# Output tiles turned by VectorE in blocks of 32 and stored in runs of 64 channels, in place of TensorE transposes and ScalarE copies

## The chip, the cores and the metric

The kernel runs on one core of a Trainium2 chip. The metric is the device time of one execution in microseconds; the median of three runs before the change is 3709.78 us (3707.08 to 3710.58).

## What is computed

Two blocks, the second fed by the first. B is 4, S is 12480, D is 128, the hidden width of the second block is 2048; all arrays are float32, except that the two large weights arrive as float64.

```python
# first block: a long convolution along S, by FFT in the reference
h_mlp = np.maximum(pos_emb @ w1, 0.0) @ w2
h_filt = h_mlp * np.exp(-0.01 * pos)[:, None]
u = x * v
y = np.fft.irfft(np.fft.rfft(u, n=2*S, axis=1) * np.fft.rfft(h_filt, n=2*S, axis=0)[None], n=2*S, axis=1)[:, :S]
x1 = (x * y).reshape(B * S, D)
# second block: 49920 tokens
h = x1 @ w_in
out = (h * np.cos(h)) @ w_out
```

## The kernel before

**Stages.** The first 330 us make the filter, its spectrum and the first transform of batch 0. From then on two streams are woven together: the convolution of the four batches (a generator, `convolutions`, that is stepped by `convolve`), and the second block, tile by tile. The convolution of a batch has forward passes (f1, f2), an inverse pass i1, and the last inverse step i2 in 30 groups. Group g of batch b gives four positions n2 for each of R = 104 values n1; it is written to the scratch tensor `zd` as 104 rows of 4 x 128 floats (`i2_out`). In i2 of batches 1 to 3 each group loads a table tile `tm` (312 KB, L673), with two buffers in batches 1 and 2 and three in batch 3; in batch 0 most of them are computed in place. Batch 3 is done at about 3065 us; from there on only the second block runs.

**A tile of the second block** is 128 rows of `zd`, so 512 tokens. There are 98: the first has 104 rows, the last 88, the 96 between have 128. Each goes through 16 steps c (one 128-wide slice of the hidden width per step):

- `moe_load` (L724) reads the rows into `tile`, 128 partitions x 512 floats, one DMA on SyncE's queue (L727).
- `moe_turn` (L730) turns them by four TensorE transposes (helper line L136) into a bank `cv`, and ScalarE copies them to `at` (L737).
- `moe_up` (L740) multiplies by a slice of `w_in` into a bank `ph` (helper line L132); ScalarE and VectorE reduce the argument of the cosine (L748, L749); `moe_act` (L753) takes the sine on ScalarE (L754) and the product on VectorE (L755), after which the bank is free. There are three banks in the pool `ps_h`.
- `moe_sums` (L757) on GpSimd and `moe_down` (L770) on TensorE apply `w_out` to pairs of slices with 7 products in place of 8 into two accumulators. The output block has 4 sub-blocks: two halves of the channels (64 each) by two halves of the tokens.
- `moe_evict` (L785) combines the accumulators on VectorE into `ot`, 128 x 4 x 128, one block each for channels-and-half of the tokens, the last combinations being L798, L800 and L801.
- `moe_back` (L804) turns the four blocks of `ot` by TensorE transposes (L136) into a bank of `ps_h`, and ScalarE copies the bank to `ob` (L811). `ob` has the name `tile` too, with one buffer, so the input tile and the output tile share one place in SBUF.
- `moe_store` (L814) writes `ob` to the output, one DMA (L822) for every piece of the tile that lies in one group of 104 rows: two or three for a full tile. A run in DRAM is 256 floats (two neighbouring positions, 1 KB).

**The order** is written out by hand in the loop from L988. In step c = 8 of tile n stand, in this order for every engine: `moe_down` of seven steps before, `moe_turn` of tile n+1, `moe_back` of tile n-1, one step of the convolution, `moe_up`; in step 10 `moe_store` of tile n-1; in step 14 `moe_load` of tile n+2, which uses the buffer that the store reads. All loads and stores go through SyncE's queue, in program order: `x`, `v` and `xs` loads (L386), `w` and `h` of the forward pass (L595, L597), `tm` (L673), `zd` (L515, L727) and the output (L822). An issue whose data or buffer isn't ready holds back everything behind it.

**w_out** is converted from float64 bits in eight pieces beside i1 of batch 0 (`float32_join` L159, whose last product on GpSimd is L166), and four combinations of its blocks are added at L938.

Of the kernel before, what the change touches and what calls it, by code (L numbers as in the profile page):

```python
# [9 lines left out]
F32 = mybir.dt.float32  # L10
# [3 lines left out]
ALU = mybir.AluOpType  # L14
PSUM = bass.MemoryType.PSUM
DRAM = bass.MemoryType.DRAM

P = 128
# [15 lines left out]
def kernel(  # L34
# [46 lines left out]
    nc = tc.nc  # L81

    B, S, D = x.shape
    FO = pos_emb.shape[1]
    DFF = moe_w_in.shape[1]
    N1, N2 = 96, 120
# [11 lines left out]
    CB = D // 2  # L98
# [4 lines left out]
    G = BANK // D  # L103
    UA = 2
# [3 lines left out]
    assert G == 2 * UA and H % UA == 0 and N2 % G == 0  # L108
    LAG = 7
    WCOL = 256  # L110

    dram = ctx.enter_context(tc.tile_pool(name="dram", bufs=1, space=DRAM))
    hd = dram.tile([N1 // 2, N2, 2, CB, 4], F32, name="hd")
    zd = dram.tile([NROWS, G, D], F32, name="zd")
# [19 lines left out]
    def transpose(dst, src, ident):  # L134
        n = src.shape[0]
        nc.tensor.transpose(dst, src, ident[0:n, 0:n])  # L136


    def float32_parts(pool, raw, factor):
        lo, hi = raw[:, :, 0], raw[:, :, 1]  # L140

        power = pool.tile([P, WCOL], U32, name="power", bufs=2)
        nc.vector.tensor_scalar(out=power[:, :], in0=hi, scalar1=20, scalar2=0x7FF,
# [5 lines left out]

        sig = pool.tile([P, WCOL], U32, name="sig", bufs=2)  # L150
        nc.vector.tensor_scalar(out=sig[:, :], in0=hi, scalar1=0xFFFFF, scalar2=0x100000,
                                op0=ALU.bitwise_and, op1=ALU.bitwise_or)
        high = sig[:, :].bitcast(F32)
        nc.scalar.activation(high, sig[:, :], AF.Copy, scale=factor * 2.0 ** -20)
        low = pool.tile([P, WCOL], F32, name="low", bufs=1)
        nc.scalar.activation(low[:, :], lo, AF.Copy, scale=factor * 2.0 ** -52)
# [3 lines left out]
    def float32_join(dst, raw, power, high):  # L160
        nc.vector.scalar_tensor_tensor(
            out=power[:, :], in0=raw[:, :, 1], scalar=0x80000000, in1=power[:, :],
            op0=ALU.bitwise_and, op1=ALU.bitwise_or)
        factor = power[:, :].bitcast(F32)
        there = factor if dst.space == DRAM else dst
        nc.gpsimd.tensor_tensor(there, high, factor, op=ALU.mult)  # L166
        if dst.space == DRAM:
            nc.sync.dma_start(dst, there)

    in_words = moe_w_in.bitcast(U32).rearrange("d (f w) -> d f w", w=2)  # L170
    out_words = moe_w_out.bitcast(U32).rearrange("(c p) (q w) -> p c q w", p=P, w=2)
    in_pieces = [(slice(c, c + WCOL), in_words[:, c:c + WCOL, :])
                 for c in range(0, DFF, WCOL)]
    out_pieces = [(c // 2, out_words[:, c:c + 2, :, :]) for c in range(0, NFC, 2)]

    def convert_units(pool, pieces, factor):

        raws, half = [], None
        for i in range(len(pieces) + 1):
            while len(raws) < min(i + 2, len(pieces)):  # L180
                raws.append(pool.tile([P, WCOL, 2], U32, name="raw", bufs=3))
                nc.sync.dma_start(raws[-1][:, :, :], pieces[len(raws) - 1][1])
            yield
            if i > 0:
                float32_join(pieces[i - 1][0], raws[i - 1], *half)
            if i < len(pieces):
                half = float32_parts(pool, raws[i], factor)
# [190 lines left out]
    def n2s(g):  # L378

        a = g * UA  # L380
        return [*range(a, a + UA), *range(N2 - UA - a, N2 - a)]
# [253 lines left out]
    def i1_units(bank):  # L635
        with tc.tile_pool(name="mid", bufs=2) as pool:
            def mm(j, ps, i):
                if i == 0:
                    ps = bank()
                i1_mm(ps, j, i)  # L640
                return ps

            yield from units(CB, I1_STEPS, lambda j: None, mm,
                             lambda j, ps: i1_evict(pool, ps, j), 2)
# [73 lines left out]
    def first_row(n):  # L718
        return min(R + (n - 1) * P, NROWS) if n else 0

    def rows_of(n):
        return first_row(n + 1) - first_row(n)

    def moe_load(pool, n):  # L724
        m, row = rows_of(n), first_row(n)
        zb = pool.tile([P, G, D], F32, name="tile", bufs=1)
        nc.sync.dma_start(zb[0:m, :, :], zd[row:row + m, :, :])  # L727
        zbs[n] = zb

    def moe_turn(pool, n):  # L730
# [54 lines left out]
    def moe_evict(pool, n, second, ot=None):  # L785
        r = rows_of(n)
        acc = sums.pop((n, second))

        def twice(a):
            return bass.AP(tensor=a.tensor, offset=a.offset, ap=[a.ap[0], [0, 2], a.ap[1]])  # L790

        if not second:
            ot = pool.tile([P, 4, P], F32, name="ot", bufs=1)
            nc.scalar.copy(out=ot[:, 2, 0:r], in_=acc[:, 0, 0:r])
            nc.vector.tensor_tensor(ot[:, 0:2, 0:r], acc[:, 1:3, 0:r], twice(ot[:, 2, 0:r]),
                                    op=ALU.add)
            return ot
        nc.vector.tensor_tensor(ot[:, 2:4, 0:r], acc[:, 0:2, 0:r], twice(ot[:, 0, 0:r]),  # L798
                                op=ALU.add)
        nc.vector.tensor_tensor(ot[:, 0, 0:r], acc[:, 1, 0:r], ot[:, 2, 0:r], op=ALU.add)  # L800
        nc.vector.tensor_tensor(ot[:, 2:4, 0:r], acc[:, 2:4, 0:r], ot[:, 2:4, 0:r], op=ALU.add)  # L801
        return ot

    def moe_back(pool, n, ot):  # L804
        m = rows_of(n)
        pt = ps_h.tile([P, BANK], F32, name="ph")
        places = pt[:, :].rearrange("p (h i e d) -> p h e i d", h=2, e=2, d=CB)
        for i, block in enumerate((1, 2, 3, 0)):
            transpose(places[0:m, i // 2, i % 2], ot[:, block, 0:m], ident)
        ob = pool.tile([P, G, D], F32, name="tile", bufs=1)  # L810
        nc.scalar.copy(out=ob[0:m, :, :].rearrange("p g d -> p (g d)"), in_=pt[0:m, :])  # L811
        return ob

    def moe_store(n, ob):  # L814
        row = first_row(n)
        while row < first_row(n + 1):
            b, g, n1 = row // R // NG, row // R % NG, row % R
            count = min(R - n1, first_row(n + 1) - row)
            first, _, second, _ = n2s(g)
            start = out[b * S + n1 * N2 + first, :]  # L820
            at = row - first_row(n)
            nc.sync.dma_start(  # L822
                bass.AP(tensor=start.tensor, offset=start.offset,
                        ap=[[N2 * D, count], [(second - first) * D, 2], [1, UA * D]]),
                ob[at:at + count, :, :].rearrange("p (h n) d -> p h (n d)", h=2))
            row += count

    with tc.manual_schedule():
        with tc.tile_pool(name="psum", bufs=8, space=PSUM) as psum, \
# [14 lines left out]
            with tc.tile_pool(name="layers", bufs=1, side="right") as pool:  # L844
# [14 lines left out]
                ident = pool.tile([P, P], F32, name="ident")  # L859
# [44 lines left out]
            def beside(units, pieces, factor, more=lambda pool: iter(())):  # L904
                with tc.tile_pool(name="convert", bufs=1) as pool:
                    convert, other = convert_units(pool, pieces, factor), more(pool)
                    for i, _ in enumerate(units):
                        if i % 14 == 0:
                            next(convert, None)
                        elif i % 5 == 0:  # L910
                            next(other, None)
                    for _ in [*convert, *other]:
                        pass
# [12 lines left out]
            for kept, here in ((rowsd, rows), (twd, tw_t)):  # L926
                nc.sync.dma_start(here[:, :, :], kept[:, :, :])
            ident = wpool.tile([P, P], F32, name="ident")
            make_identity(nc, ident)
            w_in_sb = wpool.tile([D, DFF], F32, name="w_in_sb")  # L930
            w_out_sb = wpool.tile([P, NFC // 2, 7, CB], F32, name="w_out_sb")
            nc.sync.dma_start(w_in_sb[:, :], wind[:, :])
            beside(i1_units(bank),
                   [(w_out_sb[:, p, 0:4, :].rearrange("p q d -> p (q d)"), w) for p, w in out_pieces],
                   2.0 * math.pi, some_groups)
            for dst, first_, second_, op in ((4, 1, 3, ALU.add), (5, 4, 0, ALU.subtract),
                                             (1, 0, 1, ALU.subtract), (6, 2, 5, ALU.subtract)):
# [34 lines left out]
        def load(n):  # L972
            while made[0] * R < first_row(n + 1):
                next(conv)
            moe_load(mpool, n)
# [12 lines left out]
        for i in range(len(steps) + LAG):  # L988
# [5 lines left out]
            if i < len(steps):  # L994
                n, c = steps[i]
# [22 lines left out]
        for n in sorted(ots):  # L1018
            moe_store(n, moe_back(mpool, n, ots[n]))
# [28 lines left out]
```

## Time and profile before

| | |
|---|---|
| median of three runs | 3709.78 us |
| the profiled execution | 3712.07 us, span 3710.0 us |
| mean granted TensorE clock | 0.993 of full speed |
| mean DMA rate over the span | 75 GB/s, 16 engines' share 25.7% |
| DMA packets | 209708, of them under 512 B 17111 |

The span is the time between the first and the last instruction; an engine's share is its busy time over the span. In the groups, a row gives the line, the engine, the operation, what it writes and reads with the shape, how often, the busy time as a union in us, the mean of one in ns, and the idle time of the engine ahead of it with what ended it. In the waits, a row gives who waited for whom, the total in us, how often and the longest. In the timeline, a row gives start and duration in us; SPq is SyncE issuing a DMA.

The stages of the two streams, from the windows:

| stretch, us | what runs beside the tiles | TensorE busy | DMA share |
|---|---|---|---|
| 330 to 580 | i2 of batch 0 | 236.0 of 250 | 0.52 |
| 1140 to 1405 | i2 of batch 1 | 263.8 of 265 | 0.51 |
| 2040 to 2290 | i2 of batch 2 | 247.0 of 250 | 0.57 |
| 2925 to 3065 | i2 of batch 3 | 140.0 of 140 | 0.59 |
| 3065 to 3700 | nothing | 633.5 of 635 | 0.08 |

### The profile page before, as it was taken

The page shows a single profiled execution, that of the slowest core. Times are in us where ns is not written, and L with a number is a line of the kernel's source. Part 1 is how long each engine was busy: PE and PEld are TensorE (multiplying, and loading weights), DVE is VectorE, ACT ScalarE, POOL GpSimd, SP SyncE. Part 2 cuts the span into 40 slices and gives each one's busy share as a digit, 9 for nine tenths or more (in the row PEclk, how much of TensorE's full clock was granted, in tenths as well). Part 3 has the DMA queues.
Part 4 walks back from the last instruction along what each step waited for, and adds up shares of the span by engine and source line. Part 5 has one row for each costly group of instructions (what it writes and reads, how often), then busy time and mean ns, then how long its engine had stood idle before and what let it go on. Part 6 is the DMA issues. An engine that isn't in the chain of part 4 may idle for free.

```text
span 3710.0 us, 101707 instructions
## 1 busy us (share of the span) xinstructions
PE 3620.5 (98%) x40810; PEld 2565.9 (69%) x40810; DVE 2823.2 (76%) x5373; ACT 2201.2 (59%) x4396; POOL 2792.2 (75%) x3271
## 2 busy tenths in 40 slices
PE   8898999999999999999999999999999999999999
PEld 6777776766668776766667776766667786666666
DVE  6587886588887776588887777578887667777777
ACT  4456666665554556655555455665555446666666
POOL 7667987588883887588874788578885447887877
PEclk9999999999999999999999999999999999999999
DMA  6253551012212651012210663012220361000000
GB/s 169 72 181 101 162 152 56 23 53 74 70 55 62 170 165 43 22 58 70 74 51 17 165 168 91 19 43 72 73 65 21 83 168 29 19 20 23 18 24 14
DMA packets 209708, 279.63 MB, mean 75 GB/s; under 512 B 17111, under 2 KB 146535, under 8 KB 209111
## 3 DMA queue, kind: packets, MB, share of 16 engines
q1 hardware_dynamic: 209239, 273.12, 25.7%
q8 instruction: 325, 5.32, 0.6%
q14 instruction: 144, 1.18, 0.1%
HBM read 193.64 MB, written 79.42 MB: 74 GB/s over the span
## 4 chain that ended last, share of the span: by engine, by line
PE 84%; DVE 4%; ACT 1%; POOL 1%; issue 1%; DMA 0%; ACTq 0%; POOLq 0%; DVEq 0%; SPq 0%
PE ph L132 30%; PE cv L132 18%; PE accb L780 17%; PE acca L780 13%; PE cv L419 3%; PE cv L136 1%; DVE gt L755 1%; DVE gt L749 1%; PE ph L136 1%; ACT gt L748 1%; POOL ts L763 0%; DVE xt L405 0%; POOL slots L411 0%; ACT tile L811 0%; DVE t L474 0%
## 5 line engine op out<-in xcount | busy, mean ns | idle before, releaser
L748 ACT ACTIVATE gt<-ph 128x512 int32<-128x512 f32 (+1 forms) x1380 | 823.0, 596 | 1147.4 <-PE ph L132 1085.7
L749 DVE SCALAR_TENSOR_TENSOR gt<-ph,gt 128x512 f32<-128x512 f32 (+1 forms) x1380 | 949.1, 688 | 718.5 <-ACT gt L748 715.6
L763 POOL TENSOR_TENSOR ts<-gt 128x512 f32<-128x512 f32 (+2 forms) x784 | 1007.0, 1284 | 580.0 <-PE accb L780 511.6
L132 PE MATMUL ph<-at,w_in_sb 128*64 128x512 f32 (+1 forms) x5520 | 1427.2, 592 | 13.8 <-ACT tile L811 6.5
L754 ACT ACTIVATE gt<-gt 128x512 f32<-128x512 f32 (+1 forms) x1568 | 971.7, 620 | 3.6 <-DVE gt L749 2.9
L755 DVE TENSOR_TENSOR gt<-ph,gt 128x512 f32<-128x512 f32 (+1 forms) x1380 | 936.5, 679 | 0.0
L780 PE MATMUL accb<-ts,w_out_sb 128*64 128x128 f32 (+2 forms) x9408 | 649.2, 272 | 0.0
L767 POOL TENSOR_TENSOR ts<-gt,ts 128x256 f32<-128x256 f32 (+2 forms) x784 | 575.5, 734 | 61.5
L766 POOL TENSOR_TENSOR ts<-ts,gt 128x256 f32<-128x256 f32 (+2 forms) x784 | 574.9, 733 | 61.4
L780 PEld LDWEIGHTS acca<-gt,w_out_sb 128*64 128x64 f32 x6272 | 398.4, 137 | 268.1 <-issue 231.7
L780 PEld LDWEIGHTS accb<-ts,w_out_sb 128*64 128x64 f32 x9408 | 543.0, 137 | 0.0
L780 PE MATMUL acca<-gt,w_out_sb 128*64 128x128 f32 (+2 forms) x6272 | 479.0, 272 | 0.0
L780 PEld LDWEIGHTS accb<-gt,w_out_sb 128*64 128x64 f32 x3136 | 224.6, 137 | 254.9 <-issue 198.7
L132 PEld LDWEIGHTS ph<-at,w_in_sb 128*64 128x64 f32 x5520 | 353.1, 137 | 33.8 <-ACT tile L811 14.7
L475 POOL TENSOR_TENSOR slots<-slots,t 120x256 f32<-120x256 f32 x384 | 281.6, 740 | 118.4 <-DVE t L474 69.5
L132 PEld LDWEIGHTS cv<-slots,tm 96*64 96x64 f32 (+1 forms) x3840 | 245.6, 128 | 126.9 <-issue 114.2
L780 PE MATMUL accb<-gt,w_out_sb 128*64 128x128 f32 (+1 forms) x3136 | 310.6, 273 | 4.5 <-DVE ot L801 2.9
L780 PE MATMUL acca<-ts,w_out_sb 128*64 128x128 f32 (+1 forms) x3136 | 308.3, 272 | 1.5 <-POOL ts L766 1.2
L132 PE MATMUL cv<-slots,tm 96*64 96x128 f32 (+1 forms) x3840 | 278.1, 287 | 8.8 <-POOL tm L307 5.6
L132 PEld LDWEIGHTS cv<-cs,slots 120*64 120x64 f32 (+1 forms) x3072 | 167.9, 125 | 61.1 <-issue 59.1
L780 PEld LDWEIGHTS acca<-ts,w_out_sb 128*64 128x64 f32 x3136 | 201.0, 137 | 3.0 <-POOL ts L766 2.7
L132 PE MATMUL cv<-slots,w 124*56 124x256 f32 (+1 forms) x1152 | 190.7, 407 | 1.9 <-ACT at L737 1.9
(133 smaller groups left out, 3793.2 us busy)
## 6 DMA issues: line engine op xcount, KB each, us to landing
h<-hd SPq DMA_DIRECT2D x144, 240.0 KB
tm<-td SPq DMA_DIRECT2D x96, 312.0 KB
xt<-in_x_dram SPq DMA_DIRECT2D x120, 208.0 KB
vt<-in_v_dram SPq DMA_DIRECT2D x120, 208.0 KB
xs<-in_x_dram SPq DMA_DIRECT2D x120, 208.0 KB
zd<-xs SPq DMA_DIRECT2D x119, 208.0 KB
tile<-zd SPq DMA_DIRECT2D x96, 256.0 KB
w<-wd SPq DMA_DIRECT2D x144, 116.2 KB
```

Source lines behind the costliest of these rows:

```text
L132: nc.tensor.matmul(dst[lo:hi], left[:, lo:hi], right, start=start, stop=stop)
L136: nc.tensor.transpose(dst, src, ident[0:n, 0:n])
L419: nc.tensor.matmul(dst[lo:hi], u[:, b, lo:hi, i], c1[0:u.shape[0], r:r + 2, :].rearrange("p r k -> p (r k)"), start=True, stop=True)
L475: nc.gpsimd.tensor_tensor(y[:, r], y[:, r], t[:, r], op=op)
L748: nc.scalar.activation(turns, ph[:, 0:m], AF.Identity, bias=phase)
L749: nc.vector.scalar_tensor_tensor(out=part, in0=ph[:, 0:m], scalar=phase, in1=turns, op0=ALU.add, op1=ALU.subtract)
L754: nc.scalar.activation(part, part, AF.Sin, scale=scale)
L755: nc.vector.tensor_tensor(part, ph, part, op=ALU.mult)
L763: nc.gpsimd.tensor_tensor(ts[:, 0:2, 0:half], gt[:, :, half:2 * half], gt[:, 0, 0:2 * half].rearrange("p (h n) -> p h n", h=2), op=ALU.sub ...
L766: nc.gpsimd.tensor_tensor(t[2], t[1], b11, op=ALU.add)
L767: nc.gpsimd.tensor_tensor(t[3], b21, t[2], op=ALU.subtract)
L780: nc.tensor.matmul(acc[h * CB:(h + 1) * CB, place, 0:r], w_out_sb[:, pair, weight, :], right[:, h * r:(h + 1) * r], start=(pair == 0 and i ...
```

## The change

The output tile of a full tile (128 rows) is turned by two VectorE transposes, each of 128 x 256 floats, which turn every block of 32 x 32 by itself. After that a partition holds 32 rows' places for one quarter of the 128 output partitions, so for each position it has runs of 64 channels. Three things are changed to fit: the blocks of `w_out` are written in another order (`float32_join`, L934), `ot` has five slots so that the four results lie side by side, and a full tile is loaded by four DMAs of 32 partitions that take every fourth row. The store of a piece becomes eight DMAs: four partition quarters (64 channels each) by two position pairs, with runs of 64 floats (256 B) in DRAM. The first and the last tile, which are not full, go through TensorE transposes and ScalarE's copy as before, and are loaded and stored as before.

```diff
@@ float32_join
-        there = factor if dst.space == DRAM else dst
-        nc.gpsimd.tensor_tensor(there, high, factor, op=ALU.mult)
         if dst.space == DRAM:
-            nc.sync.dma_start(dst, there)
+            nc.gpsimd.tensor_tensor(factor, high, factor, op=ALU.mult)
+            nc.sync.dma_start(dst, factor)
+            return
+        for c in range(2):
+            h, f = (a[:, c * D:(c + 1) * D].rearrange("p (s e d) -> p s e d", s=2, e=2)
+                    for a in (high, factor))
+            nc.gpsimd.tensor_tensor(dst[:, c], h, f, op=ALU.mult)
@@ moe_load
-        nc.sync.dma_start(zb[0:m, :, :], zd[row:row + m, :, :])
+        if m == P:
+            for j in range(P // TURNED):
+                start = zd[row + j, :, :]
+                nc.sync.dma_start(
+                    zb[j * TURNED:(j + 1) * TURNED, :, :].rearrange("p g d -> p (g d)"),
+                    bass.AP(tensor=start.tensor, offset=start.offset,
+                            ap=[[P // TURNED * G * D, TURNED], [1, G * D]]))
+        else:
+            nc.sync.dma_start(zb[0:m, :, :], zd[row:row + m, :, :])
@@ moe_evict
-            ot = pool.tile([P, 4, P], F32, name="ot", bufs=1)
+            ot = pool.tile([P, 5, P], F32, name="ot", bufs=1)
...
-        nc.vector.tensor_tensor(ot[:, 0, 0:r], acc[:, 1, 0:r], ot[:, 2, 0:r], op=ALU.add)
+        nc.vector.tensor_tensor(ot[:, 4, 0:r], acc[:, 1, 0:r], ot[:, 2, 0:r], op=ALU.add)
@@ moe_back
+        ob = pool.tile([P, G, D], F32, name="tile", bufs=1)
+        if m == P:
+            turned = ob[:, :, :].rearrange("p (h j) (q e d) -> p h e (j q) d", h=2, q=2, e=2)
+            for h in range(2):
+                nc.vector.transpose(
+                    turned[:, h],
+                    ot[:, 1 + 2 * h:3 + 2 * h, :].rearrange("p e (j t) -> p e j t", t=TURNED))
+            return ob
         pt = ps_h.tile([P, BANK], F32, name="ph")
...
@@ moe_store
+            nj, run = P // TURNED, UA * D * TURNED // P
+            for i in range(nj):
+                low = i * TURNED + at // nj
+                for h, n2 in enumerate((first, second)):
+                    start = out[b * S + n1 * N2 + n2, :]
+                    nc.sync.dma_start(
+                        bass.AP(tensor=start.tensor, offset=start.offset + i * run,
+                                ap=[[nj * N2 * D, count // nj], [N2 * D, nj], [1, run]]),
+                        ob[low:low + count // nj, :, :].rearrange(
+                            "p (h j) (q d) -> p h (j q) d", h=2, q=2)[:, h])
```

`TURNED` is 32.

## The prediction

> **What bounds the kernel now.** I read the page's part 1 (busy shares), then part 4 (the chain that ended last), then the groups with shapes kept apart.
>
> ```profile
> span 3710.0 us, 101707 instructions
> ...
> PE 3620.5 (98%) x40810; PEld 2565.9 (69%) x40810; DVE 2823.2 (76%) x5373; ACT 2201.2 (59%) x4396; POOL 2792.2 (75%) x3271
> ...
> PE 84%; DVE 4%; ACT 1%; POOL 1%; issue 1%; DMA 0%; ACTq 0%; POOLq 0%; DVEq 0%; SPq 0%
> ```
>
> TensorE is busy 98% of the span and is 84% of the chain; no other engine is above 76%, and DMA is 0% of the chain. So a microsecond taken from TensorE's own order is a microsecond, as long as nothing new makes it wait. Next, the rows that the change touches, from the groups:
>
> ```profile
> L136 PE MATMUL ph<-ident,ot 128*128 128x128 f32 x384 | 57.7, 273 | 0.0
> L811 ACT COPY tile<-ph 128x512 f32<-128x512 f32 x96 | 56.8, 592 | 0.7 <-PE ph L136 0.7
> L801 DVE TENSOR_TENSOR ot<-accb,ot 128x256 f32<-128x256 f32 x96 | 40.7, 424 | 3.3
> L800 DVE TENSOR_TENSOR ot<-accb,ot 128x128 f32<-128x128 f32 x96 | 28.0, 292 | 3.3
> ```
>
> The first row is the removed work: 384 transposes, 4 for each of the 96 full tiles, 57.7 us of TensorE (the 273 ns overlap, so the union counts). The second, ScalarE's copy, is 56.8 us on an engine at 59%. From the waits of TensorE:
>
> ```profile
> PE ph L132 <- ACT tile L811: 6.5, 9, 0.7
> ```
>
> TensorE stood 6.5 us because the copy L811 held a bank of ps_h, or ScalarE, before the next matmuls.
>
> **Gain.** 57.7 us of transposes plus 6.5 us of that wait: 64.2 us. What follows TensorE's transposes in its order are matmuls that stand ready (the row L132 ph waits 12 us in all 5424), so the time is not caught by the next wait. ScalarE's 56.8 us count nothing.
>
> **VectorE.** Two transposes per tile of 128x256 f32, SBUF to SBUF, 192 in all. The trace has none; the nearest rows are 292 ns (L800, 128 elements) and 688 ns (L749, 512 elements), and I take 0.42 us, the 256-element row L801: 0.84 us per tile, between 0.58 and 1.38. Their place in VectorE's order is ahead of L749 of step c=8; they wait for TensorE's transposes of the next input tile, which free the one buffer called tile. One tile in the last stage, in order of time:
>
> ```profile
> 3308.24 0.66 PE L136 MATMUL cv<-ident,tile 128*128 128x128 f32 x4
> ...
> 3308.74 0.60 PE L136 MATMUL ph<-ident,ot 128*128 128x128 f32 x4
> 3308.78 0.68 DVE L755 TENSOR_TENSOR gt<-ph,gt 128x512 f32<-128x512 f32 x1
> ...
> 3309.42 0.59 ACT L811 COPY tile<-ph 128x512 f32<-128x512 f32 x1
> ...
> 3310.03 0.79 SPq L822 DMA_DIRECT2D out_dram<-tile  x2
> ...
> 3311.08 0.69 DVE L749 SCALAR_TENSOR_TENSOR gt<-ph,gt 128x512 f32<-128x512 f32 x1 [1.62 <-ACT gt L748]
> ...
> 3312.86 0.34 SPq L727 DMA_DIRECT2D tile<-zd  x1
> ```
>
> L755 ends at 3309.46 and L749 starts 1.62 us later, held by ScalarE and so by TensorE. With the output's transposes (0.60 us) gone, this comes 0.60 earlier: 1.02 us are free, and 0.84 fit. At 1.38, L749 would be 0.36 us late; queued behind it is L755 of step 7, which frees a bank that TensorE asks for about one step (1.6 us here) later. So the cost is 0 up to about 2.6 us per tile; without that cover it would be 96 x 0.84 = 81 us. In steps beside the convolution the gap is similar (1.22 and 1.62 us in the ones I read). The Trainium skill, "VectorE: DVE Perf Modes", section on the three transpose paths, gives 311 ns for 128x128 bf16 on VectorE; an estimate from it, four such per tile, is 1.24 us, under 2.6, so the sum would be the same; no run here shows it.
>
> **SyncE's queue.** This is the cost. A full tile falls into 2 or 3 pieces at the 104-row groups (207 pieces for the 96 full tiles); each piece was one store and is now 8, so 1656 for 207; each full load is 4 for 1, 288 more. The L822 rows take 282/375/1637 ns (minimum, median, maximum), 0.36 to 0.46 us from one start to the next. A new store has at most 104 runs of 256 B where an old one had up to 208 of 1 KB. I take 0.40 us. So a tile holds the queue 14 x 0.40 = 5.6 us longer (8.4 with 3 pieces). SyncE issues in order: what stands behind comes late. Who needs it soon? I compared, for each load, issue with first use: xs, h and the input tile have 10.9 us or more, w 8.6, xt and vt mostly over 9.9, and tm, the table of the last inverse step, about 7. An example, first SyncE, then TensorE:
>
> ```profile
> 1284.58 0.77 SPq L822 DMA_DIRECT2D out_dram<-tile  x2
> 1285.44 0.37 SPq L673 DMA_DIRECT2D tm<-td  x1
> ```
> ```profile
> 1292.46 1.15 PE L132 MATMUL cv<-slots,tm 96*64 96x128 f32 x16
> ```
>
> This tm is used 7.0 us after its issue; by the packet records it lands after 4.1 (median 3.2), so 2.9 us are spare, and 5.6 us of stores make TensorE wait 2.7. There are 13 store bursts in the stages where tm is reloaded (1140 to 1405, 2040 to 2290, 2925 to 3065 us). I carried the whole queue forward: each issue keeps the moment its wait ended, or follows its forerunner; 7 more stores per piece and 3 more per load; a landing 3.3 us after issue; a load that is later than its first user stops TensorE for the difference. With 0.33 us per store that costs 12 us, with 0.40 27 us (20 of the 27 in nine tm loads, 7 in five w loads), with 0.50 64, with 0.60 119, with 0.74 210. I take 27.
>
> The bounds of the issue: below, 0.33 (the 282 ns minimum and a pause); above, rows of other queues:
>
> ```profile
> 1.24 0.60 SPq L849 DMA_DIRECT2D w_sb<-in_w_dram  x1
> ...
> 3.78 7.40 SPq L329 DMA_DIRECT2D pe<-in_pos_emb_dram  x10
> ```
>
> The first moves 64 runs of 256 B and held SyncE 0.60 us; the second took 0.74 us each with 480 runs of 512 B, while the DMA engines were full. Both lie in the first 12 us, where xt's issues too take 0.38 us or more, for a median of 0.32 over the run; the store's own row is the nearest.
>
> **DMA engines.** 1024 packets of 256 B per tile for 256 of 1 KB. In the packet records 128 packets of 256 B (reads) took 18 ns each, 512 B 37, 1 KB 57: 64 per engine are 1.2 us by the first, 2.4 by the second. Per store an engine gets at most 8, 0.14 to 0.30 us, less than the 0.40 of an issue, so SyncE sets the pace. Nothing else on the path.
>
> **At nothing:** the fifth slot of ot (same instructions); the w_out conversion, 8 GpSimd products of 821 ns cut into 16, at most 8 x 0.82 = 6.6 us more on GpSimd some 40 us ahead of their first use, below nothing excluded since the elements stay; a bank of ps_h fewer in use (its wait is counted). The store's wait on VectorE in place of ScalarE ends at about the same moment (3310.3 for 3310.0).
>
> **Sum** on the profiled execution: 3712.07 - 64.2 + 27 = 3674.9; it lay 2.3 us above the median 3709.78, so 3672.6, and I say 3672.
>
> **Rivals.**
> - Hidden: the stores slip into SyncE's idle time. For it: SyncE waits 1033 us at L822 for data alone. Against: the waits lie in the stages without tm loads. 3709.8 - 64.2 = 3646; with 0.33 us 3658.
> - **Slower: the queue.** One mechanism: a run of 16 to 24 stores issues, or drains, at 0.50 us or more each, and the tm and w loads behind it stop TensorE by more than 64 us. 0.60 (the w_sb row) gives 3710 - 64 + 119 = 3765, 0.74 gives 3856. For: those two rows, and single issues up to 1.6 us beside heavy traffic. Against: they are startup rows, and 0.37 is the store's own. Drain decides if a 256 B write takes over 50 ns (8 x 50 = 0.40). The Trainium skill, "DMA: Bandwidth & Descriptors", Specifications, says that below 512 B the DMA engine reads, modifies and writes: a rule against this change that would work just there. The trace has 256 B reads alone, at 18 ns; a read and a write at that price (36 ns) would still be hidden.
> - VectorE transposes far dearer than any row of their size, over 2.6 us per tile; each further microsecond costs up to 96 us: at 4 us, 3672 + 1.4 x 96 = 3806.
> - The change not doing what it says: excluded for full tiles, as the branch on 128 rows takes 96 of 98.
>
> **Chances.** Forecast (3650 to 3700) 0.48; hidden 0.18; queue at 0.50 or more 0.25; VectorE 0.09. About 0.2% (7 us) is what a measurement can tell from no change. The queue case starts at break-even, so 0.06 of it is "same": faster 0.66, same 0.06, slower 0.28. The range 3638 to 3770 takes in the first two and the queue up to 0.60, and leaves out 0.19.
>
> **What would show it.** Transposes of ot down to 8 (the two short tiles) and L811's copy to 2; a VectorE transpose row x192 near 420 ns; L749's wait on ScalarE shorter; some 1660 stores near 0.3 to 0.4 us; TensorE newly waiting for DMA tm<-td, about 20 us in the three stages, and none in the last one from 3065 on, where a tile falls from 27.4 to 26.8 us. Wrong: stores at 0.5 us or more, or PE waits on DVE rows.

## The result and the profile after

The changed kernel takes 4094.83 us (median of four runs, 4090.04 to 4097.34) against 3709.86 us for the kernel before on the same chip: a ratio of 1.1038 [1.1019, 1.1057]. It is 10% slower where 1% faster was forecast, and the time lies outside the range. From the page of the changed kernel, the lines that answer to those of before (span; part 1, engines; part 4, the chain):

```profile
span 4088.3 us, 103302 instructions
...
PE 3674.8 (90%) x40426; PEld 2571.2 (63%) x40426; DVE 2877.9 (70%) x5565; ACT 2152.7 (53%) x4300; POOL 2788.8 (68%) x3279
...
PE 62%; SPq 15%; DVE 5%; DMA 4%; issue 2%; ACT 1%; POOL 1%; DVEq 0%; ACTq 0%; POOLq 0%
```

TensorE has 384 instructions fewer, as meant, and yet is busy 54.3 us longer (3620.5 before); and it stands idle for 4088.3 - 3674.8 = 413.5 us where it stood 89.5. SyncE's issuing (SPq), which was 0% of the chain, is 15% of it. The longest waits of TensorE in the changed kernel (total us, times, longest):

```profile
PE cv L133 <- DMA w<-wd: 188.3, 28, 12.0
PE cv L133 <- DMA tm<-td: 108.4, 13, 13.9
PE ph L133 <- DVE gt L768: 30.4, 9, 10.5
```

Both DMA rows are new: 296.7 us of waiting for loads. A third of the last row is a late load too: its longest wait, 10.5 us, ends at 619.4 us, just after VectorE, which feeds it, had stood 10.6 us for vt (VectorE's waits have `DVE xt L410 <- DMA vt<-in_v_dram: 10.6, 1, 10.6`). The instructions around the tile (duration minimum/median/maximum in ns, first and last start in us):

```profile
L854 SPq DMA_DIRECT2D out_dram<-tile x1656: 583/785/1748, 438.7 to 4082.3; - x184
L735 SPq DMA_DIRECT2D tile<-zd x384: 302/413/1875, 359.2 to 4002.8; - x192
L823 DVE STREAM_TRANSPOSE tile<-ot x192: 394/416/446, 431.4 to 4064.1; 128x256 f32<-128x256 f32 x192
```

The VectorE transpose costs the 0.42 us that was taken for it. A store's issue costs 0.785 us, not 0.40; from one start to the next it is 0.82 us (mean of 1548 pairs). What that does, first on SyncE's queue, then on TensorE:

```profile
1307.75 0.31 SPq L391 DMA_DIRECT2D vt<-in_v_dram  x1
1308.11 18.27 SPq L854 DMA_DIRECT2D out_dram<-tile  x24
1326.49 0.35 SPq L678 DMA_DIRECT2D tm<-td  x1
```
```profile
1316.86 1.02 PE L133 MATMUL ph<-at,w_in_sb 128*64 128x512 f32 x4
1330.26 1.94 PE L133 MATMUL cv<-slots,tm 96*64 96x128 f32 x16 [12.39 <-DMA tm<-td]
```

24 stores hold SyncE for 18.27 us; the table behind them is issued at 1326.49, lands 3.8 us later, and TensorE has waited 12.39 us for it. The sixteen products that follow take 1.94 us where the same row took 1.15 in the example of before: the clock's records in this trace show half speed from 1320.0 to 1333.7 us, so TensorE comes out of the halt at the lower clock. Over the whole span the mean granted clock is 0.950, against 0.993 before. The w loads fare alike: one that is issued at 1131.51, behind 24 stores that hold SyncE for 18.24 us, keeps TensorE waiting for 10.42 us.

### The profile page after: what moved, and what is told of

Same layout as the page of the kernel before. It is cut to its first block, busy times and chain, and to the rows that moved or that the text cites. A ratio compares the mean times of both kernels' runs of the same rounds, so it can differ in the third digit from the quotient of the medians.

```text
span 4088.3 us, 103302 instructions
## 1 busy us (share of the span) xinstructions
PE 3674.8 (90%) x40426; PEld 2571.2 (63%) x40426; DVE 2877.9 (70%) x5565; ACT 2152.7 (53%) x4300; POOL 2788.8 (68%) x3279
## 4 chain that ended last, share of the span: by engine, by line
PE 62%; SPq 15%; DVE 5%; DMA 4%; issue 2%; ACT 1%; POOL 1%; DVEq 0%; ACTq 0%; POOLq 0%
PE ph L133 21%; SPq L854 14%; PE cv L133 14%; PE accb L793 13%; PE acca L793 9%; PE cv L424 3%; DMA w<-wd 3%; DVE gt L768 2%; DVE gt L762 2%; PE cv L137 1%; DMA tm<-td 1%; ACT gt L761 1%; DVE t L479 1%; POOL ts L776 0%; DVE xt L410 0%
## 5 line engine op out<-in xcount | busy, mean ns | idle before, releaser
L133 PE MATMUL ph<-at,w_in_sb 128*64 128x512 f32 (+1 forms) x5520 | 1451.8, 604 | 31.4 <-DVE gt L768 30.4
L793 PE MATMUL accb<-ts,w_out_sb 128*64 128x128 f32 (+2 forms) x9408 | 665.3, 277 | 0.0
L793 PEld LDWEIGHTS accb<-ts,w_out_sb 128*64 128x64 f32 x9408 | 558.4, 140 | 0.0
L793 PE MATMUL acca<-gt,w_out_sb 128*64 128x128 f32 (+2 forms) x6272 | 488.9, 277 | 0.0
L133 PEld LDWEIGHTS cv<-slots,tm 96*64 96x64 f32 (+1 forms) x3840 | 254.9, 133 | 244.1 <-issue 172.8
L133 PE MATMUL cv<-slots,tm 96*64 96x128 f32 (+1 forms) x3840 | 291.2, 297 | 117.8 <-DMA tm<-td 108.4
L133 PE MATMUL cv<-slots,w 124*64 124x256 f32 (+1 forms) x1152 | 202.9, 431 | 193.7 <-DMA w<-wd 188.3
L133 PEld LDWEIGHTS cv<-slots,w 124*64 124x64 f32 (+1 forms) x1152 | 81.0, 141 | 364.0 <-DMA w<-wd 213.0
```

The lines of the kernel that those rows point to most:

```text
L133: nc.tensor.matmul(dst[lo:hi], left[:, lo:hi], right, start=start, stop=stop)
L793: nc.tensor.matmul(acc[h * CB:(h + 1) * CB, place, 0:r], w_out_sb[:, pair, weight, :], right[:, h * r:(h + 1) * r], start=(pair == 0 and i ...
```

## The experiments

Times are medians, with the ratio to the kernel before on the same chip.

**1. One store per piece.** The change's turning and loads, with the old store, one per piece (the rows land in other places of the output).

```diff
+            nc.sync.dma_start(
+                bass.AP(tensor=start.tensor, offset=start.offset,
+                        ap=[[N2 * D, count], [(second - first) * D, 2], [1, UA * D]]),
+                ob[at:at + count, :, :].rearrange("p (h n) d -> p h (n d)", h=2))
...
-            for i in range(nj):
-                low = i * TURNED + at // nj
-                for h, n2 in enumerate((first, second)):
...
```

> The changed kernel with one store per piece in the shape of before (two runs of 1 KB a row) in place of eight; VectorE's transposes, the four-way loads and everything else stay. The rows land in the wrong places of the output, so only the time is meant. Queue theory (the eight stores hold SyncE's queue and tm and w come late): the loss goes and the removed TensorE work shows, 3710 - 64 = 3646 us (3640 to 3665), no wait of TensorE for tm or w, the TensorE clock at full speed from 350 us on. Rival, VectorE's transposes or the four-way loads delay TensorE: about 4095 us stays, or at least well above 3710.

Measured: 3666.65 us, 0.9883 [0.9868, 0.9897]. The whole loss lies in the stores; without them turning on VectorE gains 43 us. That is less than the 64 forecast. From its page:

```profile
span 3664.6 us, 101692 instructions
...
PE 3578.1 (98%) x40426; PEld 2515.2 (69%) x40426; DVE 2881.6 (79%) x5565; ACT 2154.4 (59%) x4300; POOL 2792.5 (76%) x3279
```

TensorE's busy time fell by 42.4 us (3620.5 - 3578.1), not by the 57.7 of the removed row, and its idle time by 3.0. The second part can be read in the waits, first of the kernel before, then of this one:

```profile
PE cv L132 <- ACT at L737: 2.4, 9, 0.5
```
```profile
PE cv L133 <- ACT at L750: 6.3, 9, 0.9
```

The wait of 6.5 us for the output's copy L811 is gone, but the output's transposes also gave ScalarE time to copy the next input tile; without them TensorE waits for that copy, 3.9 us more.

**2 and 3. The same number of stores, of other shape.** Eight stores per piece each, to other rows than the reference has: once with 1 KB runs, once with the change's 256 B runs but with the two row levels exchanged, so that the DRAM side can't be joined into one level.

```diff
-                    start = out[b * S + n1 * N2 + n2, :]
+                    start = out[b * S + (n1 + i) * N2 + n2, :]
...
-                                ap=[[nj * N2 * D, count // nj], [N2 * D, nj], [1, run]]),
+                                ap=[[nj * N2 * D, count // nj], [1, UA * D]]),
...
```
```diff
-                                ap=[[nj * N2 * D, count // nj], [N2 * D, nj], [1, run]]),
+                                ap=[[N2 * D, count // nj], [count // nj * N2 * D, nj], [1, run]]),
```

> The changed kernel with the same eight stores per piece over the same partitions, but each partition's 256 floats go to one run of 1 KB in DRAM, so rows and partitions match one to one; the data land in the wrong places. If the price of an issue hangs on the shape (four runs for one partition): an issue takes 0.3 to 0.4 us in place of 0.79, and the queue carried forward at 0.40 gives 3710 - 64 + 27 = 3673 us. If every store of a part of the partitions costs 0.8 us whatever its shape, so that the number of issues alone counts: about 4095 us.

> The changed kernel with eight stores per piece with runs of 256 B, but the four runs of a partition go to rows that lie a quarter of the piece apart, so that the two dimensions of the DRAM side cannot be joined and both sides have the partition outermost. The rows land in the wrong places. If the price comes from the joined DRAM side (1 x 104 rows against 26 partitions): 0.3 to 0.45 us an issue and 3665 to 3700 us. If it comes from runs of 256 B, or from four runs for one partition: about 0.8 us and 4095 us, as in the changed kernel.

Measured: 3711.79 us, 1.0004 [0.9995, 1.0014], and 3714.59 us, 1.0019 [1.0009, 1.0029]: 380 us below the changed kernel, though above what was expected of either. The stores of the kernel with 1 KB runs, then of the one with 256 B runs:

```profile
L854 SPq DMA_DIRECT2D out_dram<-tile x1656: 235/329/1893, 439.7 to 3706.3; - x184
```
```profile
L854 SPq DMA_DIRECT2D out_dram<-tile x1656: 237/343/2027, 437.0 to 3702.2; - x184
```

So neither the number of stores nor the 256 B run makes an issue dear. The kernel of experiment 3 moves the same bytes in the same 98304 packets of 256 B as the changed one, and its issue takes 0.343 us where that one's takes 0.785. What differs is the order of rows: in the changed kernel row = 4 x place + block, whose two levels are one even step on the DRAM side, and the instruction there has a single level of 8 to 104 rows against partitions x 4 in SBUF; here both sides have two levels. With the single level the median issue takes between 0.59 us (64 rows) and 0.84 (104 rows). What in the issuing makes it so was not tried further and stays open.

Even at the cheap price the stores cost 3712.0 - 3664.6 = 47.4 us in experiment 3, where a price of 0.40 us was forecast to cost 27. Two rows of TensorE's waits there:

```profile
PE cv L133 <- DMA tm<-td: 20.8, 11, 3.7
PE cv L133 <- DMA w<-wd: 11.8, 9, 2.8
```

These two are 32.6 us, not far from the 27: at the price that the prediction took, its waits come out. TensorE's idle time is 36.5 us above that of the first experiment, and its busy time 10.9 us. Most of the second part is the clock: TensorE was busy for 20.1 us at half speed there and for 3.4 in the first experiment, and half of the difference, some 8 us, is what full speed would have saved (an estimate).

**4. The change's stores alone.** The kernel before, TensorE transposes and all, with the eight stores of the change (rows land elsewhere).

> The kernel before with TensorE's transposes and ScalarE's copies, its loads and its w_out order, and only the stores of the change (eight per piece, runs of 256 B); the rows land in the wrong places. Queue theory: the whole loss is here and the transposes' 64 us come on top: 4095 + 64 = about 4160 us (4110 to 4200; the TensorE work may hide part of the waits). Rival, the loss belongs to VectorE's transposes or to the loads: near 3710 us.

Measured: 4131.35 us, 1.1135 [1.1118, 1.1151]. The stores do it without the turning: TensorE waits 189.2 us for w and 102.8 for tm, as in the changed kernel.

**5. The change's stores, spread.**

```diff
...
-                if c == (NFC - 2 if n else NFC - 1) and n + 2 < NALL:
-                    load(n + 2)
+                if n > 1 and c == 1 and n + 1 < NALL:
+                    for _ in stores.pop(n - 2):
+                        pass
+                    load(n + 1)
...
-                if c == NFC // 2 + 2 and n - 1 in obs:
-                    moe_store(n - 1, obs.pop(n - 1))
+                if c == NFC // 2 and n - 1 in obs:
+                    stores[n - 1] = moe_store(n - 1, obs.pop(n - 1))
+                for left in stores.values():
+                    for _ in range(3 if c != NFC // 2 else 0):
+                        next(left, None)
...
```

> The change's own stores, 256 B runs and joined rows included, but three per step over the steps c = 9 to 15 of the tile and the first of the next, and the load behind them moved to step c = 1 of the next tile, 7 steps ahead of its use. The output is the reference's. Theory (what hurts is a burst of 16 to 24 issues at 0.83 us that the tm and w loads stand behind): each issue still takes 0.6 to 0.85 us, but a load now stands behind at most three of them, 2.5 us, less than the 2.9 us that the example tm had to spare. So nearly all DMA waits of TensorE go, the clock is back above 0.985, and the time is 3667 to 3690 us. Rival (the 256 B writes load the DMA engines or the memory, so that loads land late however they are queued): the waits for tm and w stay, over 3900 us.

Measured: 3804.35 us, 1.0251 [1.0236, 1.0267]. 290 of the 385 us are gone with the stores as dear as before (median 785 ns), so the writes as such are not the cause; but the expected time was missed by 114 us: TensorE still waits 47.3 us for tm and 33.1 for w. One stretch of the queue shows how; then TensorE:

```profile
1255.23 0.33 SPq L391 DMA_DIRECT2D xt<-in_x_dram  x1
1259.53 0.31 SPq L391 DMA_DIRECT2D vt<-in_v_dram  x1
1259.89 5.05 SPq L855 DMA_DIRECT2D out_dram<-tile  x6
...
1267.42 7.53 SPq L855 DMA_DIRECT2D out_dram<-tile  x10
1275.37 0.35 SPq L678 DMA_DIRECT2D tm<-td  x1
```
```profile
1278.68 1.20 PE L133 MATMUL cv<-slots,tm 96*64 96x128 f32 x16 [3.17 <-DMA tm<-td]
```

The issue of vt waits 4 us for its buffer, and what the following steps have put behind it collects: 6 and 10 stores in a row, not 3, and the table comes 3.17 us late. Spreading in the program is not spreading in time when the queue halts for something else. Whether the other late loads come about in the same way is not shown.

**6. Output transposes twice**, in the kernel before (same output).

```diff
-        for i, block in enumerate((1, 2, 3, 0)):
-            transpose(places[0:m, i // 2, i % 2], ot[:, block, 0:m], ident)
+        for _ in range(2):
+            for i, block in enumerate((1, 2, 3, 0)):
+                transpose(places[0:m, i // 2, i % 2], ot[:, block, 0:m], ident)
```

> The kernel before with each output tile's four TensorE transposes made twice into the same places (work added, same output), 384 more of them. Theory (four transposes in a row beside others cost 0.49 us, the start-to-start sum of the input tile's in before, 47.5 us for 97 tiles; the rest of their busy row is a turnaround of 0.16 us that is paid once per row of transposes, whoever is last in it): 3710 + 47 = 3757 us, 3752 to 3760. Rival (four cost what their busy row says, 57.7 us, and 6.5 us of waiting come with them, and the gain of turning on VectorE was lost elsewhere): 3768 to 3774 us.

Measured: 3739.0 us, 1.0075 [1.0060, 1.0090]: 28 us, less than either expected. One output tile in the timeline:

```profile
3299.80 1.04 PE L136 MATMUL ph<-ident,ot 128*128 128x128 f32 x8
```

Eight take 1.04 us where four took 0.60, so four more cost 0.44: each transpose starts 109 ns after the one before (the median of every place in the row but the last), and the 273 ns of one are mostly overlap. The edit holds for the two short tiles too, so 392 are added, not 384: 392 x 0.109 = 42.7 us. About 11 us of this are covered by a halt that stood there before (from the start of the last transpose to that of the next matmul the mean falls from 335 to 219 ns); this leaves some 3 us over the measured 28, which no row explains.

**7. Turning alone**: experiment 1 with one load per tile as before.

```diff
-            for j in range(P // TURNED):
...
+        nc.sync.dma_start(zb[0:m, :, :], zd[row:row + m, :, :])
```

> The kernel with VectorE's turning and one store per piece in the old shape, and now also one load per tile as before, so that all of the change that is left is the turning itself (rows land in other places than the reference has them). Theory (the gain was 43 us and not 64 because removed transposes were worth 0.45 us per tile): no difference from the kernel with four loads, 3663 to 3669 us. Rival (288 more loads on SyncE's queue ate the missing 20 us): 3645 to 3652 us.

Measured: 3666.95 us, 0.9879 [0.9862, 0.9895]. The four loads per tile cost nothing that can be told.

**8 and 11. Rows in runs, output as the reference's**: the input tile is loaded piece by piece, so that the store of experiment 3 puts its rows in the right places; in 8 with the stores spread as in 5, in 11 in one burst.

```diff
+            at = 0
+            while at < m:
+                count = min(m - at, R - (row + at) % R)
+                part = count * TURNED // P
+                for j in range(P // TURNED):
+                    low = j * TURNED + at * TURNED // P
+                    nc.sync.dma_start(zb[low:low + part, :, :],
+                                      zd[row + at + j * part:row + at + (j + 1) * part, :, :])
+                at += count
```

> As the spread stores, but the rows of a piece are dealt out to the four blocks of 32 partitions in runs (row = place in block + block x quarter of the piece) and not every fourth, so that the store's rows can't be joined; the loads become four per piece, 8 to 12 per tile. The output is the reference's. Theory (the price is that of the joined side): a store takes 0.26 to 0.42 us as in the kernel with rows in runs, the queue is never late, and the time is that of turning alone, 3665 to 3680 us, at or below the spread one. Rival (256 B runs are dear in themselves): as dear as the spread kernel's stores, 0.58 to 0.85 us, and the 8 to 12 loads in a row make it slower than that kernel.

> The kernel with rows in runs and loads by piece (output as the reference's), with the stores and the load at their old places, in one burst each. Theory (stores at 0.39 us from start to start in one burst still make tm and w late, and spreading them is what gained): near the 3715 us of the kernel with the same stores and four loads, a little above for the 4 to 8 loads more: 3712 to 3735 us, with 30 us or more of TensorE waiting for tm and w. Rival (loads by piece gained, not the spreading): 3690 to 3697 us as with the spreading.

Measured: 3694.18 us, 0.9951 [0.9936, 0.9965], and 3717.83 us, 1.0017 [1.0008, 1.0027]. Number 8 computes the whole output and is faster than both kernels. Its stores, and what is left of the new waits:

```profile
L858 SPq DMA_DIRECT2D out_dram<-tile x1656: 237/342/2033, 434.2 to 3682.1; - x184
```
```profile
PE cv L133 <- DMA tm<-td: 9.2, 7, 2.5
```

It stays 27.8 us above turning alone (spans of 3692.4 and 3664.6), where at most 15 were expected; 19.0 of them are TensorE's idle time. Number 11 comes out as expected, with 29.2 us of waiting for tm and w; against it, spreading is worth 24 us with cheap stores.

**9, 10 and 12. Halts without a DMA.** In the kernel before, a chain of 14, 26 or 8 VectorE additions whose result nobody uses, ahead of step 4 of 18 tiles of the last stage, to see what a halt of TensorE does to its clock.

```diff
...
+                if c == 4 and 78 <= n < 96:
+                    for _ in range(14):
+                        nc.vector.tensor_tensor(held[:, :], held[:, :], held[:, :], op=ALU.add)
```

> The kernel before with 14 idle VectorE additions of 128x128 (292 ns each by the row of that shape, 4.1 us together) put ahead of step c = 4 of the 18 tiles 78 to 95, in the last stage, where no table or w is loaded and the stores stay as before; the output is the same. It holds back VectorE's own work and so TensorE. With some 2.6 us of slack, TensorE should stand 1.5 us (0.5 to 2.5) each time, 9 to 45 us in all: 3719 to 3755 us. Theory (TensorE falls to half speed after it stood for more than 3 us): hardly any half-speed stretch, and TensorE's busy time stays within 5 us of 3620. Rival (half speed follows the stores' traffic, or any halt): the same here for the traffic, but for any halt 18 stretches.

> The same with 26 additions (7.6 us): TensorE should stand about 5 us in each of the 18 tiles, 90 us in all. Theory (a halt of over 3 us brings a stretch at half speed, whatever caused the halt): 18 such stretches of 3 to 10 us, TensorE's busy time up by about 2.2 us for each (96.7 us for 44 stretches in the changed kernel, against the one with one store per piece), so by 40 us, and a time of about 3840 us (3800 to 3860). Rival (half speed comes from the traffic of the stores or of the loads that were late, not from the halt): no stretch at half speed, busy time unchanged, and the time is up by the halts alone, about 3800 us.

> As the kernel with 14 additions, with 8 (2.3 us). There the halts came out at the length of the additions, with no slack: 18 of 4.2 us, and each was followed by a stretch at half speed. Here 18 halts of about 2.4 us, 43 us in all. Theory (only a halt of over 3 us brings half speed, apart from a few between 1.5 and 3 us: 21 of 50 in the kernels with spread or cheap stores): at most half of them are followed by a stretch, and TensorE's busy time rises by 0 to 20 us over 3620: 3750 to 3772 us. Rival (any halt does it): 18 stretches, busy time up by 38 us as with 14 and 26 additions: 3788 to 3795 us.

Measured: 3831.41 us, 1.0326 [1.0311, 1.0342]; 3894.06 us, 1.0495 [1.0477, 1.0512]; 3770.87 us, 1.0160 [1.0143, 1.0177]. The slack that the first two counted on was not there, so both came out above their ranges: the additions also hold back the emptying of an accumulator (L795), and TensorE halted for their full length. With 14 additions:

```profile
3198.23 1.03 PE L132 MATMUL ph<-at,w_in_sb 128*64 128x512 f32 x4
3203.47 0.66 PE L780 MATMUL acca<-gt,w_out_sb 128*64 128x128 f32 x8 [4.22 <-DVE ot L795]
3203.96 0.39 PE L780 MATMUL acca<-ts,w_out_sb 128*64 128x128 f32 x4
3204.18 1.86 PE L132 MATMUL cv<-at,w_in_sb 128*64 128x512 f32 x4
```

After the halt the same four matmuls take 1.86 us in place of 1.03. The last stage by windows (stretch; busy time of PE, PEld, DVE, ACT, POOL; granted clock; DMA), before, with 8 and with 26 additions:

```profile
3065.00:3700.00 635.00, 633.50 (x6955) 410.01 (x6953) 503.71 (x844) 442.69 (x819) 510.58 (x562) 1.00 0.08 20
```
```profile
3065.00:3700.00 635.00, 587.45 (x6202) 374.26 (x6198) 516.47 (x900) 402.26 (x734) 458.66 (x502) 0.98 0.07 19
```
```profile
3065.00:3700.00 635.00, 516.54 (x5272) 332.29 (x5268) 513.33 (x1020) 340.39 (x622) 389.26 (x427) 0.89 0.06 16
```

| additions | halts | half-speed stretches that follow | TensorE busy, whole run |
|---|---|---|---|
| 8 | 18 of up to 2.3 us | 9 | 3634.2 (+13.7) |
| 14 | 18 of 4.2 us | 18 | 3661.5 (+41.0) |
| 26 | 18 of 8.1 us | 18 | 3655.8 (+35.3) |

At no more DMA traffic than before, the halts alone bring half speed, and a long halt no more of it than one of 4 us: about 2 us each. The rival with the traffic is out, and so is "any halt": of the 18 halts with 8 additions, all 2.24 to 2.26 us long, half brought it and half did not, so at this length something besides the length decides, and that stays open.

## Why the prediction was wrong

**The path** was right: SyncE's queue, with w and tm behind the stores, is where the time went, and the direction is that of the rival called the queue; but even that rival's highest price, 0.74 us, gave only 3856 us. **The step that failed is the price of a store's issue**: "0.40", taken from L822 as the nearest row and with the bound of 0.74 above it; it is 0.82 us from start to start, above even that bound. The choice went by what a store moves (fewer and shorter runs than the old one), and the runs show that the price hangs on the shape of the two sides instead. The prediction's carrying forward of the queue, redone on the trace of before with 0.83 us a store, gives 250 to 280 us of waiting (an estimate): 150 to 170 in 28 loads of w and 100 to 110 in 13 of tm. The trace has 188.3 us in 28 and 108.4 in 13. So w, which at 0.40 us came second to tm, leads at this price, and for the waits it was the number put in that failed, not the carrying forward.

**The gain** of 64.2 us was 45.4 in span (experiment 1). "The union counts" was wrong: four transposes are 0.60 us of busy time, but the engine could start the next matmul earlier than their modelled end, and 0.44 us is what their removal frees. The last stage shows it: a tile there falls from 27.41 to 26.97 us, in the changed kernel too, where 26.8 was expected. And "the time is not caught by the next wait" failed by 3.9 of the 6.5 us.

**The clock was no term of the sum**: the prediction put it at nothing without naming it. TensorE has the same instructions in experiment 1 and in the changed kernel, but is busy 3578.1 and 3674.8 us: 96.7 us more. The clock's records in the trace of the changed kernel show 44 stretches at half speed after 340 us, where the kernel before has none (one at the very end of each run left out). TensorE is busy for 192.6 us within them; if the same work takes half as long at full speed, 96.3 us are the clock's (an estimate), which is the whole difference.

On the two spans: -45.4 (turning) + 327.0 (idle, 86.5 to 413.5) + 96.7 (clock) = +378.3 us, where -64.2 + 27 = -37.2 was forecast. Of the 415.5 us between them, 300.0 are waiting, 96.7 the clock and 18.8 the smaller gain. **VectorE** was right to 1% in the price and right that it is covered: no wait of TensorE in the changed kernel names L823. **The 256 B packets** were right too: they took 20 ns in the median in the changed kernel. The Trainium skill's rule ("DMA: Bandwidth & Descriptors", Specifications: below 512 B the engine reads, modifies and writes) decides nothing here: the same packets with rows in runs cost 3714.59 us against 3711.79 with 1 KB runs.

## What to carry over

Before a store is cut into more pieces, price the issue by a row of the same shape on both sides, and not by the bytes; where there is no such row, rows of other shapes give no upper bound. What stands behind a burst in a queue pays for the burst, and spreading helps only where the queue itself doesn't halt. Count removed TensorE work from start to start, not by its busy time. Count a new halt of TensorE of over 3 us at its length plus some 2 us for the half speed behind it.

## What the runs showed of the hardware

Halts and half speed, over the fourteen traces (halts of TensorE after 340 us; a halt counts as followed when half speed starts during it or within 6 us of its end): 140 of 140 halts over 3 us were followed, 29 of 54 from 2 to 3 us, 11 of 137 from 1 to 2 us. The stretches in the changed kernel last 3.4 us (3 times), 6.8 (25), 10.2 (13), 13.7 (2) and 17.1 (1), whole multiples of 3.4, but for the last one at the end of the run. The Trainium skill, "TensorE: Matmul & The Clock Gate", Part 1, gives a free-running window of 3413 ns and half rate after at least one idle window; the lengths agree, but half of the halts between 2 and 3 us brought it on as well, and there the measurement decides.

A second shape is dear in issue too: in the kernel before, the 13 stores of 64 rows took 0.61 us in the median, those of other sizes 0.30 to 0.44. The load of w_sb, which took 0.60 us and which the prediction set aside as a row of the startup, moves 64 runs as well, so its price need not come from the startup. Why 64 is dear was not tried.
